# Two interleaved attention and MLP layers on one core: unpinned norms in the MLP, weight copies moved into attention, more buffers for projected tiles, another order of the first loads

## The chip, the cores and the metric

The kernel runs on one core of a Trainium2 chip. The metric is the device time of one execution in microseconds. The kernel before took 3666.28 us (median of 3 runs, 3660.68 to 3670.13).

The engines are named as in the profile: PE is the matrix engine (TensorE), PEld its weight loads, DVE the vector engine, ACT the scalar engine, POOL is GpSimd, and SP only issues DMAs. ACT and POOL issue some DMAs too. Each engine works through its own instructions in a fixed order and waits on semaphores.

## The reference

The input x has 2048 rows of 512 numbers in float32. Two layers follow each other, with the same weights in both:

```python
def _A_ref(x, wqkv, wo):                 # 32 heads of 16
    q, k, v = split_heads(x @ wqkv)
    scores = q @ k.T * 16 ** -0.5
    return heads_to_rows(softmax(scores) @ v) @ wo
def _B_ref(x, w1, b1, w2):
    h = x @ w1 + b1                      # 512 -> 1792
    sp = log1p(exp(-abs(h))) + where(h > 0, h, 0)
    return (h * tanh(sp)) @ w2
x = x + _A_ref(_layernorm(x), A_wqkv, A_wo)
x = x + _B_ref(_layernorm(x), B_w1, B_b1, B_w2)
x = x + _A_ref(_layernorm(x), A_wqkv, A_wo)
x = x + _B_ref(_layernorm(x), B_w1, B_b1, B_w2)
```

(The helpers `split_heads` and `heads_to_rows` stand for reshapes and transposes.)

## The kernel before

**Numbers.** Matmul operands are kept as a high and a low part (two tiles of type float32r). A product is three matmuls: high by high, high by low, low by high (`mm3`, L153, whose matmuls appear in the profile as L156, L157, L158). A part pair is made by a copy on ACT and a subtraction on DVE (`split_psum`, L149; profile lines L150 and L151) or, for weights, by a copy on ACT and a subtraction on POOL (`split_load`, L105; L112, L113).

**Stages.** The 2048 rows are four chunks `c` of 512. Per layer:

1. *Norm* (`norm_parts`, L163). Statistics on DVE (L174, L175), the inverse root on POOL (L171, tile `rs`), the normalised rows `xn` (L187, DVE), four transposes per 128 rows on PE (L198, tile `tp`), and the split of the transposed tile into `th` and `tl`. A norm is a generator of five pieces: the statistics, then one piece per 128 rows. Names that end in q belong to attention's norms, names that end in m to the MLP's.
2. *Projections* (`qkv`, L445). For each of 8 column blocks `m` (0 to 3 for queries, 4 to 7 for keys) and each chunk `c`, 12 matmuls of 128x512 fill a PSUM bank; ACT and DVE split it into the tile `pt`, and ACT issues its 512 KB write to the DRAM tensor `scr` (L471). The order of the pairs (m, c) is a list (L676). `pt` has three buffers, under the tag raw. When all (0, c) and (4, c) are written, `prep_qk` (L238) loads the tiles `ks` and `qs` of the first group of heads from `scr`, half of it through SP and half through POOL. From block 6 on, `some_max` (L450) puts score matmuls `pm` (L292) and their row maxima `mxv` (L296, DVE) between the projections. Then come the V projections (`v_parts`, L492), whose result goes to DRAM and comes back as `va`.
3. *Attention* (`run`, L394), 512 steps: scores again (`sp`, `ss`), exponentials on ACT into the tiles `p` (L347, L357), the products with V (`pv`, L372), and, 28 steps ahead, the maxima. Functions in a dictionary `hooks` run after a given step. In layer 0 the weights of the later stages are split there on POOL and copied to DRAM (`split_keep`, L119).
4. *Output projection and MLP* (`wo_parts`, `mlp`). `mlp` walks over 56 pairs (c, f), f being one of 14 column blocks of 128. `hid(c, f)` (L584) does 12 matmuls and a chain of eleven instructions: `hb` (ACT, L594), `he` (DVE, L595), `he` (ACT, L596), `he` (DVE, L597), `hr` twice (ACT, L598, L599), `hb` (POOL, L600), `ah` (DVE, L602), `hb` (POOL, L603), `al` (DVE, L604). `outp` (L607) runs two pairs later (LAG) and does 12 matmuls on `ah` and `al` into `mo`. `hb` has two buffers, `he` and `hr` one.

Norms of the next chunk, and in the last chunk of layer 0 the first three norms of layer 1's attention, run beside the MLP: `spread` (L206) hangs their five pieces behind the `hid` of five neighbouring f. Layer 1's projection weights are loaded there too (L769, through ACT's queue).

**Weights.** `load_qkv` (L432) in layer 0 loads raw weights (tag raw, three buffers, shared with `pt`; the V weights use a tile of their own, `rawv`) and splits them; `keep_all` (L654) copies the split weights to DRAM through POOL, 1 MB each, from where layer 1 loads them. Weights 0 and 2 serve blocks 0, 1, 4, 5; weights 1 and 3 serve blocks 2, 3, 6, 7; weights 4 and 5 are V.

**Space.** Nearly all large tiles (`x`, `th`, `tl`, split weights, `ks`, `qs`, `va`, `p`, `v`) share one tag of 22 slots of 8 KB per partition (`b8`, L76).

**What sets the order.** The program is traced in Python; then a list scheduler plays a timing model (L778) and fixes each engine's order of instructions and which buffer a tile gets: of the instructions that are ready in the model, the one traced first goes first. `behind` (L160) pins an instruction behind the one traced just before it on its engine. In `spread` every DVE and ACT instruction of a norm is pinned (`pin=behind`); its transposes on PE and its `rs` on POOL are not.

Of the kernel before, what the change touches and what calls it, by code (L numbers as in the profile page):

```python
# [9 lines left out]
F32 = mybir.dt.float32  # L10
F32R = mybir.dt.float32r
BF16 = mybir.dt.bfloat16
AF = mybir.ActivationFunctionType
ALU = mybir.AluOpType
# [4 lines left out]
P = 128  # L19
S, D, H, DH, F = 2048, 512, 32, 16, 1792  # L20
NCH = 4
CW = S // NCH
# [17 lines left out]
AHEAD = 24  # L40
PRE = 4
FILL = 12
GSTEPS = NCH * NKT
STEPS = NG * GSTEPS
HEADS = STEPS * HG
# [7 lines left out]
def kernel(ctx: ExitStack, tc: tile.TileContext, x, wqkv, wo, w1, b1, w2, out):  # L53
    nc = tc.nc
# [5 lines left out]
    tmp = ctx.enter_context(tc.tile_pool(name="tmp", bufs=2))  # L60
# [15 lines left out]
    def b8(shape, dt, name):  # L76
        return blk.tile(shape, dt, tag="blk", name=name)
# [18 lines left out]
    def t512(tag, name, dt=F32):  # L96
        return tmp.tile([P, 512], dt, tag=tag, name=name, bufs=T_BUFS.get(tag, 2))

    kept, unkept = {}, []

    def keep(key, t):
        kept[key] = dram.tile(list(t.shape), F32R, name="w" + key)
        nc.gpsimd.dma_start(kept[key].bitcast(F32), t.bitcast(F32))

    def split_load(key, src, a, b, later, raw=None):  # L105
        t = b8([P, 2, a, b], F32R, "s" + key)
        if raw is None:
            raw = tmp.tile([P, a, b], F32, tag="raw", name="r" + key, bufs=3)
        nc.sync.dma_start(raw, src)

        def split():
            nc.scalar.activation(t[:, 0], raw, AF.Copy)  # L112
            nc.gpsimd.tensor_tensor(t[:, 1], raw, t[:, 0].bitcast(F32), op=ALU.subtract)  # L113
            unkept.append((key, t))

        later.append(split)
        return t
# [28 lines left out]
    def rows2(w, j):  # L146
        return w[ts(j, 2 * P), :].rearrange("(k p) n -> p k n", p=P), 2, w.shape[1]
# [9 lines left out]
            pe(nc.tensor.matmul(acc, ah, bl, start=False, stop=False))  # L157
            pe(nc.tensor.matmul(acc, al, bh, start=False, stop=last and i == n - 1))  # L158

    def behind(ins):  # L160
        return tc.keep_in_program_order(ins)

    def norm_parts(src, nm, got, key, tag, fine=False, pin=lambda ins: ins, pe=lambda ins: ins, halves=False):  # L163
        st = tmp.tile([P, NCH, 6], F32, tag="st", name=f"st{nm}")
        mv = tmp.tile([P, NCH, 2], F32, tag="mv", name=f"mv{nm}")
        ve = tmp.tile([P, NCH], F32, tag="ve", name=f"ve{nm}")
        rs = tmp.tile([P, NCH], F32, tag="rs", name=f"rs{nm}")

        def rstd(t, n):
            pin(nc.vector.tensor_scalar(ve[:, t : t + n], mv[:, t : t + n, 1], EPS, None, op0=ALU.add))  # L170
            nc.gpsimd.tensor_tensor(rs[:, t : t + n], ve[:, t : t + n], mhalf[:, t : t + n], op=ALU.pow)  # L171

        for t in range(NCH):
            pin(nc.vector.bn_stats(st[:, t], src[:, t]))  # L174
            pin(nc.vector.bn_aggr(mv[:, t], st[:, t]))  # L175
            if fine:
                rstd(t, 1)
        if not fine:
            rstd(0, NCH)
        yield  # L180
        th = b8([P, KT, CW], F32R, f"th{nm}")
        tl = b8([P, KT, CW], F32R, f"tl{nm}")
        got[key] = (th, tl)
        for t in range(NCH):
            xn = t512("f", f"xn{nm}{t}")
            pin(
                nc.vector.tensor_scalar(  # L187
                    xn, src[:, t], mv[:, t, 0:1], rs[:, t : t + 1], op0=ALU.subtract, op1=ALU.mult
                )
            )  # L190
            if halves:
                yield
            if tag == "mx":
                tp = ps.tile([P, 2, 512], F32, tag=tag, name=f"tp{nm}{t}")[:, 0]
            else:
                tp = pbank(tag, f"tp{nm}{t}")
            for k in range(KT):
                pe(nc.tensor.transpose(tp[:, ts(k, P)], xn[:, ts(k, P)], ident))  # L198
            split_psum(th[:, :, ts(t, P)], tl[:, :, ts(t, P)], tp.rearrange("p (k n) -> p k n", k=KT), pin)
            yield  # L200
# [3 lines left out]
            pass  # L204

    def spread(hooks, at, src, nm, got, key):  # L206
        parts = norm_parts(src, nm, got, key, "acc", pin=behind)
        for c, f in at:
            hooks.setdefault((c, f), []).append(lambda: next(parts, None))

    class Attention:
# [60 lines left out]
        def max_mm(self, s, half):  # L272
# [3 lines left out]
            g, qb = divmod(b, NCH)  # L276
            u, i = divmod(2 * i + half, GSTEPS // 4)
            qt, n = divmod(i, NCH)
            l = self.l
            if half == 0 and s % GSTEPS >= GSTEPS // 2 and g + 1 < NG:  # L280
                if s % GSTEPS == GSTEPS // 2:
                    self.parts = self.prep_qk(g + 1)
# [111 lines left out]
        def run(self, hooks, pre, fill):  # L394
# [49 lines left out]

    def qkv(l, wts, tt, order, late, due):  # L445
        scr = [dram.tile([2, P, S], F32R, name=f"scr{l}{m}") for m in range(2 * NCH)]
        att = Attention(l, scr)
        ahead = [0]

        def some_max():  # L450
            if ahead[0] < AHEAD + PRE:
                att.tick()
                for n in range(2):
                    att.max_mm(ahead[0], n)
                ahead[0] += 1

        done = 0
        for m, c in order:
            if c not in tt:
                late()  # L460
            w = wts[m // 2]
            pt = tmp.tile([P, 2, CW], F32R, tag="raw", name=f"pt{l}{m}{c}", bufs=3)
            th, tl = tt[c]
            acc = pbank("s", f"qk{l}{c}{m}")
            mm3(
                acc,
                [(w[:, 0, k, ts(m % 2, P)], w[:, 1, k, ts(m % 2, P)], th[:, k], tl[:, k]) for k in range(KT)],
                pe=att.pe,
            )
            split_psum(pt[:, 0], pt[:, 1], acc)  # L470
            nc.scalar.dma_start(  # L471
                scr[m][:, :, ts(c, CW)].bitcast(F32).rearrange("a p n -> p a n"), pt.bitcast(F32)
            )
            for fn in due.get((m, c), []):
                fn()
            if m in (0, 4):
                done += 1
                if done == 2 * NCH:
                    for _ in att.prep_qk(0):
                        pass  # L480
                    att.chained = True
            elif done == 2 * NCH and m in MAX_M:
                some_max()
        i = 0
        for c in range(NCH - 1):
            for _ in v_parts(l, c, wts, tt, att, False):
                i += 1
                if i % 3 == 0:
                    some_max()
        return att  # L490
# [154 lines left out]
        return xc  # L645

    wts, tt, late = {}, {}, None
    splits = []

    def split_all():  # L650
        while splits:
            splits.pop(0)()

    def keep_all():  # L654
        while unkept:
# [5 lines left out]
    for c in range(NCH):  # L661
        parts = norm_parts(xc[c], f"q0{c}", tt, c, "mx", c == 0)
        next(parts)
        if c == 0:
            split_all()
        for _ in parts:
            pass
        if c == 0:
            load_qkv(0, wts, (1, 3), splits)
            split_all()  # L670
        if c + 2 < NCH:
            xc.append(load_x(c + 2))
    for l in range(2):
        due = {}
        if l == 0:
            order = [(0, 0), (4, 0), (1, 0), (5, 0), (0, 1), (4, 1), (1, 1), (0, 2), (4, 2), (0, 3), (4, 3)]  # L676
            due[1, 2] = [lambda: load_qkv(0, wts, (4, 5), splits)]
            due[2, 0] = [split_all]
            due[6, 0] = [keep_all]
        else:  # L680
            order = [(0, 0), (0, 1), (0, 2), (4, 0), (4, 1), (4, 2), (1, 0), (1, 1), (1, 2), (5, 0), (0, 3), (4, 3)]
        order += [(m, c) for m in (1, 5, 2, 6, 3, 7) for c in range(NCH) if (m, c) not in order]
# [17 lines left out]
        def at(s, fn):  # L700
            hooks.setdefault(s, []).append(fn)

        if l == 0:
            jobs = [(f"wo{i}", rows2(wo, i)) for i in range(2)]
            jobs += [(f"w1{i}", cols(w1, i)) for i in range(7)] + [(f"w2{i}", rows2(w2, i)) for i in range(7)]
            for i, (key, src) in enumerate(jobs):
                split_keep(hooks, 20 + 26 * i, key, *src)
# [57 lines left out]
        wts, tt = {}, {}  # L765
# [38 lines left out]
```

## Time and profile before

| what | us |
|---|---|
| median of 3 runs | 3666.28 |
| the profiled execution | 3669.02 |
| its span | 3667.2 |
| PE busy (28784 matmuls) | 3568.3 (97%) |
| DVE busy | 2968.4 (81%) |
| ACT busy | 2522.6 (69%) |
| POOL busy | 567.0 (15%) |
| layer 0: projections and V until attention is under way | 0 to about 214 |
| layer 0: attention | to about 1470 |
| layer 0: MLP, chunks end at | 1600, 1691, 1772, 1868 |
| layer 1: projections and attention | to about 3297 |
| layer 1: MLP, chunks end at | 3426, 3516, 3598, 3664 |

How to read it: a row of a timeline has start, duration, engine, line, operation, written tile <- read tiles, shapes, and in brackets how long the engine had been idle and who ended that. A window's row has, after its length, the busy time of PE, PEld, DVE, ACT and POOL with the number of instructions, then the granted clock of PE (1.00 is full speed), the mean share of the 16 DMA engines that was busy, and the GB/s that they moved. The end of a chunk is the end of its last addition to x (L621).

### The profile page before, as it was taken

What the parts mean: (1) busy time and instruction counts of PE and PEld (TensorE: products, weight loads), DVE (VectorE), ACT (ScalarE), POOL (GpSimd) and SP (SyncE); (2) the same over time, 40 slices, a digit from 0 to 9 for tenths busy, and PEclk for the clock granted to TensorE, in tenths of its full rate; (3) what the DMA queues carried; (4) which work ended last, traced back from release to release, by engine and by line L of the source; (5) the groups of instructions that cost most, each with busy time, mean ns of one, the idle gap of its engine ahead of it and who ended that gap; (6) DMA issues with size and microseconds to landing.
All of it is one profiled execution on the core that took longest, in us unless ns stands there. A gap on an engine that the chain in (4) does not pass through costs nothing. (4 is left out here: it accounts for less than half of the span.)

```text
span 3667.2 us, 69407 instructions
## 1 busy us (share of the span) xinstructions
PE 3568.3 (97%) x28784; PEld 1950.0 (53%) x28784; DVE 2968.4 (81%) x2978; ACT 2522.6 (69%) x3475; POOL 567.0 (15%) x589
## 2 busy tenths in 40 slices
PE   7999999999999999999889999999999999999999
PEld 6644444444444444877666444444444444447777
DVE  4779999999999994656647799999999999945565
ACT  2168888888888887344421788888888888873444
POOL 2200101001010002444430000000000000024455
PEclk9999999999999999999999999999999999999999
DMA  7641313313121124500154311112021221246000
GB/s 226 211 109 36 80 47 72 67 38 77 48 62 48 51 77 68 177 35 12 46 172 162 74 31 34 37 39 43 19 45 28 45 40 25 77 75 192 13 12 24
DMA packets 128707, 254.07 MB, mean 69 GB/s; under 512 B 18680, under 2 KB 62584, under 8 KB 114568
## 3 DMA queue, kind: packets, MB, share of 16 engines
q1 hardware_dynamic: 101896, 174.58, 19.5%
q0 software_dynamic: 8224, 35.21, 3.5%
q10 hardware_dynamic: 18272, 39.85, 2.9%
q8 instruction: 226, 3.70, 0.4%
q14 instruction: 89, 0.73, 0.1%
HBM read 148.38 MB, written 99.09 MB: 67 GB/s over the span
## 5 line engine op out<-in xcount | busy, mean ns | idle before, releaser
L296 DVE TENSOR_REDUCE mxv<-pm 128x2 f32<-128x1024 f32 x2048 | 2389.0, 1220 | 181.1 <-PE pm L292 132.4
L347 ACT ACTIVATE p<-sp 128x1024 f32<-128x1024 f32 x1366 | 1397.3, 1023 | 19.4 <-PE sp L346 12.0
L372 PE MATMUL pv<-p,va 128*32 128x128 f32 (+3 forms) x16048 | 1166.9, 392 | 0.0
L292 PE MATMUL pm<-ks,qs 48*128 48x512 f32 x4096 | 1109.1, 446 | 0.2
L357 ACT ACTIVATE p<-ss 128x512 f32<-128x512 f32 x1364 | 815.2, 598 | 384.7 <-PE ss L356 288.7
L346 PE MATMUL sp<-qs,ks 50*128 50x512 f32 x2732 | 739.6, 446 | 4.8 <-ACT p L347 3.3
L292 PEld LDWEIGHTS pm<-ks,qs 48*128 48x128 f32 x4096 | 460.7, 184 | 360.9 <-issue 236.6
L372 PEld LDWEIGHTS pv<-p,va 128*32 128x32 f32 x16048 | 368.3, 108 | 499.0 <-issue 418.4
L356 PE MATMUL ss<-qs,ks 50*128 50x512 f32 x1364 | 611.9, 449 | 0.1
L356 PEld LDWEIGHTS ss<-qs,ks 50*128 50x128 f32 x1364 | 252.0, 185 | 305.7 <-ACT p L357 210.1
L346 PEld LDWEIGHTS sp<-qs,ks 50*128 50x128 f32 x2732 | 277.0, 183 | 202.4 <-ACT p L347 117.6
L319 POOL CAST np<-nf 16x128 fp32r<-16x128 f32 x64 | 17.9, 280 | 2335.9 <-ACT nf L318 2317.8
L603 POOL TENSOR_TENSOR hb<-hb,hr 128x512 f32<-128x512 f32 x112 | 161.6, 1442 | 159.5 <-DVE ah L602 135.7
L600 POOL TENSOR_TENSOR hb<-hb,he 128x512 f32<-128x512 f32 x112 | 155.5, 1389 | 194.1 <-DVE he L597 192.7
L594 ACT ACTIVATE hb<-h,b1t 128x512 f32<-128x512 f32 x112 | 77.0, 687 | 152.8 <-DVE al L604 117.0
L604 DVE TENSOR_TENSOR al<-hb,ah 128x512 fp32r<-128x512 f32 x112 | 112.7, 1007 | 81.9 <-POOL hb L603 81.9
L598 ACT ACTIVATE hr<-he 128x512 f32<-128x512 f32 x112 | 70.8, 632 | 133.1 <-POOL hb L603 76.5
L150 ACT ACTIVATE pt<-qk 128x512 fp32r<-128x512 f32 x64 | 37.9, 597 | 176.9 <-PE qk L158 117.2
L596 ACT ACTIVATE he<-he 128x512 f32<-128x512 f32 x112 | 70.8, 632 | 95.2 <-DVE he L595 95.2
L602 DVE TENSOR_TENSOR ah<-hb,hr 128x512 fp32r<-128x512 f32 x112 | 76.9, 686 | 54.9 <-ACT hr L599 45.3
L597 DVE SCALAR_TENSOR_TENSOR he<-he 128x512 f32<-128x512 f32 x112 | 79.1, 706 | 49.4 <-ACT he L596 46.7
L595 DVE TENSOR_SCALAR he<-hb 128x512 f32<-128x512 f32 x112 | 67.6, 604 | 59.0 <-ACT hb L594 28.5
(225 smaller groups left out, 3289.3 us busy)
## 6 DMA issues: line engine op xcount, KB each, us to landing
scr<-pt ACTq DMA_DIRECT2D x64, 512.0 KB
qs<-scr SPq DMA_DIRECT2D x180, 128.0 KB
ks<-scr SPq DMA_DIRECT2D x180, 128.0 KB
vscr<-v SPq DMA_DIRECT2D x32, 512.0 KB
va<-vscr SPq DMA_DIRECT2D x64, 256.0 KB
oscr<-ot SPq DMA_DIRECT2D x64, 256.0 KB
ww<-sw POOLq DMA_DIRECT2D x14, 1024.0 KB, 5.2
qs<-np SPq DMA_DIRECT2D x512, 2.0 KB
```

What stands on the lines that cost most here:

```text
L292: nc.tensor.matmul(pm[:, e], qs[u][rows, q0 : q0 + P], ks[u][rows, ts(n, 512)], start=True, stop=True)
L296: nc.vector.tensor_reduce(self.mxs[b][:, 2 * u : 2 * u + 2, qt, n], pm, axis=AX.X, op=ALU.max)
L346: self.pe(nc.tensor.matmul(sp[:, e], k, q, start=True, stop=True))
L347: nc.scalar.activation(self.pts[-1][:, 0:n], sp[:, 0:n], AF.Exp, scale=SCALE)
L356: self.pe(nc.tensor.matmul(sp, k, q, start=True, stop=True))
L357: nc.scalar.activation(self.pts[i // 3][:, 2], sp, AF.Exp, scale=SCALE)
L372: nc.tensor.matmul(self.accs[b][ts(h, VW), cols], self.va[b // NCH][:, kt, h, :], self.pts[j][:, e, cols], start=kt == 0 and q0 == 0, stop ...
L594: nc.scalar.activation(hb, acc, AF.Identity, bias=b1t[:, f : f + 1])
L597: nc.vector.scalar_tensor_tensor(e, e, 2.0, e, op0=ALU.add, op1=ALU.mult)
L600: nc.gpsimd.tensor_tensor(hb, hb, e, op=ALU.mult)
L603: nc.gpsimd.tensor_tensor(hb, hb, r, op=ALU.mult)
L604: nc.vector.tensor_tensor(al, hb, ah.bitcast(F32), op=ALU.subtract)
```

## The change

Four things change.

*Norms.* In `spread`, the norm pieces are no longer pinned.

*Copies to DRAM.* `keep` pins its DMA behind what was traced before it on POOL. `keep_all` no longer runs in the projections (behind the first splits, and after pair (6, 0)) but as a hook of attention's step KEEP = 2, for all six weights together.

*Buffers.* Every other `pt` no longer comes from the three buffers of tag raw, but is half of a slot of the 22.

*First loads.* Loads and splits of `split_load` are pinned on SP, ACT and POOL. Weights 1 and 3 are loaded after pair (4, 0), the second projection, instead of right after the first norm, and split after (0, 3), the tenth; the V weights are loaded after (4, 2), the ninth, and split after (5, 2), the fifteenth, instead of after (1, 2) and (2, 0).

```diff
+KEEP = 2
...
     def keep(key, t):
         kept[key] = dram.tile(list(t.shape), F32R, name="w" + key)
-        nc.gpsimd.dma_start(kept[key].bitcast(F32), t.bitcast(F32))
+        behind(nc.gpsimd.dma_start(kept[key].bitcast(F32), t.bitcast(F32)))
...
-        nc.sync.dma_start(raw, src)
+        behind(nc.sync.dma_start(raw, src))
 
         def split():
-            nc.scalar.activation(t[:, 0], raw, AF.Copy)
-            nc.gpsimd.tensor_tensor(t[:, 1], raw, t[:, 0].bitcast(F32), op=ALU.subtract)
+            behind(nc.scalar.activation(t[:, 0], raw, AF.Copy))
+            behind(nc.gpsimd.tensor_tensor(t[:, 1], raw, t[:, 0].bitcast(F32), op=ALU.subtract))
             unkept.append((key, t))
...
     def spread(hooks, at, src, nm, got, key):
-        parts = norm_parts(src, nm, got, key, "acc", pin=behind)
+        parts = norm_parts(src, nm, got, key, "acc")
...
-        for m, c in order:
+        spare = []
+        for n, (m, c) in enumerate(order):
...
-            pt = tmp.tile([P, 2, CW], F32R, tag="raw", name=f"pt{l}{m}{c}", bufs=3)
+            if n % 2:
+                if not spare:
+                    two = b8([P, 2, 2, CW], F32R, f"pt{l}{m}{c}")
+                    spare += [two[:, 0], two[:, 1]]
+                pt = spare.pop(0)
+            else:
+                pt = tmp.tile([P, 2, CW], F32R, tag="raw", name=f"pt{l}{m}{c}", bufs=3)
...
         if c == 0:
-            split_all()
+            split_all(splits)
         for _ in parts:
             pass
-        if c == 0:
-            load_qkv(0, wts, (1, 3), splits)
-            split_all()
...
-            due[1, 2] = [lambda: load_qkv(0, wts, (4, 5), splits)]
-            due[2, 0] = [split_all]
-            due[6, 0] = [keep_all]
+            due[4, 0] = [lambda: load_qkv(0, wts, (1, 3), splits)]
+            due[4, 2] = [lambda: load_qkv(0, wts, (4, 5), later)]
+            due[0, 3] = [lambda: split_all(splits)]
+            due[5, 2] = [lambda: split_all(later)]
...
         if l == 0:
+            at(KEEP, keep_all)
```

More of the change, by code (lines that the diff above doesn't have):

```diff
@@ L97, in t512, with behind @@
         return tmp.tile([P, 512], dt, tag=tag, name=name, bufs=T_BUFS.get(tag, 2))
+    def behind(ins):
+        return tc.keep_in_program_order(ins)
     kept, unkept = {}, []
@@ L158, in mm3 @@
             pe(nc.tensor.matmul(acc, al, bh, start=False, stop=last and i == n - 1))
-    def behind(ins):
-        return tc.keep_in_program_order(ins)
     def norm_parts(src, nm, got, key, tag, fine=False, pin=lambda ins: ins, pe=lambda ins: ins, halves=False):
@@ L647, with split_all @@
     wts, tt, late = {}, {}, None
[L648 to L652, printed above, removed]
+    splits, later = [], []
+    def split_all(todo):
+        while todo:
+            todo.pop(0)()
     def keep_all():
```

## The prediction

> **What bounds the kernel now.** I read the page first, then PE's timeline for every gap of over a quarter of a microsecond, then the other engines' timelines around each gap, and the windows for stage totals. The strip of 40 slices says where to look:
>
> ```profile
> PE   7999999999999999999889999999999999999999
> DVE  4779999999999994656647799999999999945565
> PEclk9999999999999999999999999999999999999999
> ```
>
> TensorE (PE) is the bound nearly everywhere: in the attention stretches each 100 us window shows it 99.2 to 99.4 us busy. The page's PE row, 3568.3 of 3667.2 us, leaves 98.9 us idle. My list of gaps puts 27.9 us of it before 200 us, 35.0 between 1400 and 2060, and 13.0 after 3230. The diff touches exactly these places. (The digit of the clock strip is too coarse; the windows below show the clock.)
>
> The projections of layer 0:
>
> ```profile
> 34.23 0.60 ACT L150 ACTIVATE pt<-qk 128x512 fp32r<-128x512 f32 x1 [6.27 <-DMA scr<-pt]
> 36.75 1.94 PE L198 MATMUL tpq<-ident,xnq 128*128 128x128 f32 x8 [5.89 <-DVE tlq L151]
> 95.69 0.60 ACT L150 ACTIVATE pt<-qk 128x512 fp32r<-128x512 f32 x1 [8.26 <-DMA scr<-pt]
> 97.06 0.79 PE L156 MATMUL qk<-thq,sqkv 128*128 128x512 f32 x1 [4.50 <-DVE pt L151]
> 30.00:47.00 17.00, 10.42 (x41) 8.50 (x40) 10.00 (x19) 4.44 (x8) 0.00 (x0) 0.70 0.45 177
> 85.00:104.00 19.00, 11.52 (x31) 8.36 (x31) 2.77 (x4) 4.65 (x7) 3.04 (x3) 0.73 0.91 264
> ```
>
> ACT stands still because a `pt` buffer (three in tag raw) is still being written to DRAM. Everything behind it on ACT stands too, and PE follows. The seventh figure of a window (0.70, 0.73) is the granted clock: after such a gap, matmuls start 0.43 us apart instead of 0.23.
>
> The MLP, first in its last chunk of layer 0, then in an undisturbed place:
>
> ```profile
> 1801.15 0.69 DVE L604 TENSOR_TENSOR al<-hb,ah 128x512 fp32r<-128x512 f32 x1 [1.40 <-POOL hb L603]
> 1801.76 0.54 DVE L187 TENSOR_SCALAR xnq<-x,mvq,rsq 128x512 f32<-128x512 f32 x1
> 1802.60 0.43 DVE L595 TENSOR_SCALAR he<-hb 128x512 f32<-128x512 f32 x1 [0.30 <-ACT hb L594]
> 1801.88 0.69 ACT L594 ACTIVATE hb<-h,b1t 128x512 f32<-128x512 f32 x1 [2.92 <-DVE al L604]
> 1612.65 1.77 DVE L604 TENSOR_TENSOR al<-hb,ah 128x512 fp32r<-128x512 f32 x1 [1.19 <-POOL hb L603]
> 1772.00:1868.00 96.00, 79.76 (x341) 58.70 (x340) 56.29 (x106) 37.70 (x60) 34.71 (x27) 0.98 0.24 88
> ```
>
> A pinned norm piece (`xnq`) must follow `al`, the last step of an activation chain, and here the next chain starts only after it: chains stand one behind the other. `al` comes every 7.4 us (1793.73, 1801.15, 1808.57). Undisturbed (1604 to 1628), two chains overlap, `al` comes about every 5.3 us, and PE, which needs 24 x 0.227 = 5.45 us per step, is 25.00 of 25.00 us busy. So a norm in the MLP turns a PE-bound step into a chain-bound one. PE has two steps of slack (LAG); the fourth or fifth such step stalls it.
>
> **The change, part by part.** The sum is made against the profiled execution, 3669.0 us (span 3667.2), which lies 2.7 us above the median of 3666.3.
>
> *A. First stall, 30 to 47 us.* Idle 5.89 + 0.69. Slow clock: two batches of eight transposes at 1.94 instead of 1.04 us (1.8), and about ten matmuls 0.2 us late each (2.0). Together 10.4. More `pt` buffers take the ACT wait away. The four copies of weights to DRAM (4 MB, issued at 14.96 and 22.82) that the fourth `pt` had to share the DMA engines with are gone from here; SP now issues x before the second weights. POOL loses two 2.4 us subtractions ahead of the norm of chunk 1 (its `rsq` stood until 21.82). What is late next: the transposes of chunk 1 go in two batches through two PSUM buffers, with an ACT and a DVE copy between, some 2.4 us. **-8**.
>
> *B. Second stall, 85 to 104 us.* Idle 2.98 + 4.50; slow clock 6 + 15 matmuls x 0.2 = 4.2; together 11.7. Here the loads of `ks` and `qs` (issued 72 to 85, landing in 9 to 13 us) share the DMA engines with the `pt` writes; a write issued at 79.16 frees its buffer at 95.6. Sixteen microseconds are six projections of 2.73 us: three buffers fail, seven or more suffice. But the first score matmul needs `ks`. Before, 23 us passed from the last needed write (72.1) to the last landing (about 95). After, nine projections (24.5 us) lie between, with denser writes. I give 4 us back. **-7.7**; bounds 0 and -11.7.
>
> The staged weights 1 and 3 hold two of three raw buffers while projections 2 to 9 run, so every other `pt` has one buffer and 5.5 us to come back. A write issued at 70.4 had landed by 72.1; with 1.4 us from ACT to issue this fits, at nothing. If it took the 10.5 us of the first write (23.7 to 34.2), A would be lost.
>
> *The moved loads and splits.* SP issues weights 1 and 3 behind x2 and x3 (they took 7.8 us of SP's time at 5.15, waiting for a raw buffer) and the V weights ahead of the `ks` issues instead of behind them (87.44): two half-megabyte loads each, the first near 25 us, where four copies no longer are, the second near 55, where the DMA share was 0.55. ACT gets two copies of 1.06 us after projection (0, 3), with three PSUM banks as cover: 5 us of projections against 2.1. POOL subtracts 2 x 2.4 us ahead of its half of the `ks` issues, done some 7 us after that projection; the last needed write lands some 6 us after it (2.73 + 1.4 + 1.7), so POOL's issues come 1 us late, inside the 4 us of B. The V splits go behind those issues; their first reader stood at 147. Nothing more for these; without the PSUM cover it would be 2 us.
>
> *C. Layer 1 projections.* PE waits for `pt` 2.20 + 1.69 + 1.80 us (1917 to 1927). Weights live six slots here as before, and the norm inputs are gone, so the extra buffers have room. **-5.5**.
>
> *D. First MLP chunk, both layers.* Layer 0: 0.39 + 2.75 + 0.90 + 0.67 idle, and 1576 to 1592 at clock 0.89 (1.8 lost): 6.5. Layer 1: 0.39 + 2.75 + 0.69, and 3400 to 3417 at 0.80 (3.4 lost): 7.2. Unpinned, statistics can go where DVE idles (9.5 of 20 us in 1580 to 1600) and `xn` need not follow `al`. I take four fifths: **-11**.
>
> *E. Last chunk of layer 0.* Three norms stand in it; 96.0 - 79.8 = 16.2 us idle. The norms add 12 x (0.54 + 0.69) + 3 x 3.4 = 25 us of DVE work to 14 steps, 1.8 us each; with the 3.5 us of an undisturbed step DVE reaches 5.3 of the 6.0 us that PE then needs. It fits, barely, so I take two thirds: **-11**.
>
> *F. Middle chunks, both layers.* Gaps of 3.9 us each; half: **-4**.
>
> *G. Copies moved into attention.* Six copies issue on POOL behind what is traced there (0.57 us each, 3.4 in all); queued behind them is the next `np`, which has 50 us. They land in 5.2 us (`ww`, in attention) to 9.1 us (`wqkv`, before) each, 31 to 55 us in series, and until then four to six of 22 slots stay taken as the first `p` tiles need them. Fourteen copies of that size already run in layer 0's attention with PE at 99.2%; six at once the trace does not show. Between 0 and 15 us (31 us at half speed) I take **+3**, near the row of attention.
>
> Sum: -8 - 7.7 - 5.5 - 11 - 11 - 4 + 3 = -44.2, or 3624.8 on the profiled execution, **3622** on the median.
>
> [...] A 2.98 us gap at 85.2 was followed by matmuls 0.43 us apart from 89.80 on. [...]
>
> `al` took 1.77 us beside POOL's multiply at 1612.58, and 0.69 us at 1801.15 with POOL idle. [...]
>
> **Rivals.**
> 1. *The pins cost nothing of their own.* The overlapped `al` is 1.1 us longer; with norms that makes 5.3 + 1.1 = 6.4 us of DVE per step, over PE's 6.0, and D to F bring little. Against: 1604 to 1629 is full in spite of the collisions. -21 + 3: about 3648.
> 2. *The load of `ks` is the bound.* B is given back in full at the first score matmul, the rest stands: 3630.
> 3. *Slower: norm copies in ACT's queue wait for PE.* The instruction order is fixed at compile time from modelled times. If a copy of a transposed tile stands ahead of an activation, and its transpose stands behind an output matmul that waits for that activation's chain, each piece costs up to the longest gap before an output matmul, 2.75 us at 1582. Nine spread norms have 36 pieces: 99 us for the 38 lost now (D to F), +61, less 18 from A, B, C and G: 3709. It decides above (38 + 18) / 36 = 1.6 us a piece. At 1579.76 such a copy delayed the next activation by only 0.6 us.
>
> **How the numbers follow.** Forecast 0.60 (3600 to 3644); rival 1 0.18, rival 2 0.12, rival 3 0.10. Everything recovered (10.4 + 11.7 + 5.7 + 13.7 + 18, E with its clock of 0.98, + 7.8) is 67: 3599, so the range starts at 3598. It ends at 3656, where the MLP gives nothing and half of the projections' gain is gone; that leaves out rival 3 and part of rival 1. A measurement can tell about 0.3%, 11 us. Faster by more: 0.60 + 0.14 + 0.11 = 0.85; within: 0.04 + 0.01 + 0.03 = 0.08; slower: 0.07.
>
> **What would show it.** A, B: no ACT wait on `scr<-pt` before 105 us, clock 1.00 after 25 us, attention starting 12 to 20 us earlier. D, E: `al` every 5.3 to 6.2 us in norm stretches, the last chunk of layer 0 in 83 to 88 us instead of 96. G: PE near 99% in the first 100 us of attention. It is wrong if `al` still comes every 7 us, or PE waits for `ks` or for `p` for over 10 us.

## The result and the profile after

The changed kernel takes 3619.99 us (median of 4 runs, 3618.25 to 3625.20), beside 3667.55 us for the kernel before in the same session (4 runs): a ratio of 0.9876, 95% interval 0.9858 to 0.9893, or about 46 us less. Predicted were 3622, with 3598 to 3656 as the range. The profiled execution took 3625.2 us (span 3623.4), 43.8 us less than the profiled one before; the sum of the prediction's terms was -44.2. The lines of the changed kernel lie 1 to 8 further down in the file (`al` is L612, `xn` L188, the copies and subtractions of `pt` L154 and L155).

The page's strip first. Two of its 40 digits for PE were 8 before, for the slices from 1742 to 1925 us; now only the first slice is below 9:

```profile
PE   7999999999999999999999999999999999999999
```

The strip can't show the projections. PE's timeline does, with ACT's longest wait ahead of a `pt` copy and the write that ACT issues just before it, then the same two windows as before:

```profile
15.88 1.94 PE L199 MATMUL tpq<-ident,xnq 128*128 128x128 f32 x8 [5.08 <-DVE tlq L155]
18.51 1.65 PE L160 MATMUL qk<-thq,sqkv 128*128 128x512 f32 x3 [0.69 <-ACT thq L154]
38.55 1.08 PE L199 MATMUL tpq<-ident,xnq 128*128 128x128 f32 x4 [2.34 <-DVE mvq L176]
85.84 0.80 PE L160 MATMUL qk<-thq,sqkv 128*128 128x512 f32 x1 [3.08 <-DVE pt L155]
84.00 0.37 ACTq L479 DMA_DIRECT2D scr<-pt  x1
84.47 0.60 ACT L154 ACTIVATE pt<-qk 128x512 fp32r<-128x512 f32 x1 [9.23 <-DMA qs<-scr]
30.00:47.00 17.00, 12.88 (x55) 9.97 (x55) 11.67 (x26) 5.17 (x10) 1.77 (x2) 0.80 0.09 33
85.00:104.00 19.00, 18.16 (x74) 13.95 (x75) 8.57 (x11) 6.03 (x10) 6.55 (x3) 0.91 0.89 268
```

The waits of 5.89 and 4.50 us are gone, but three gaps of over 2 us are left behind the first transposes: 5.08 us at 15.88, before the first projection (2.89 before, and 2.90 in a second profile of the changed kernel, e12 below), a new one of 2.34 at 38.55, behind statistics of a later chunk, and 3.08 at 85.84, where one of 2.98 stood before. The first window went from 10.42 to 12.88 busy microseconds at a clock of only 0.80; the second from 11.52 to 18.16.

The MLP's last chunk of layer 0, DVE's timeline and the window from chunk end to chunk end:

```profile
1783.09 0.68 DVE L612 TENSOR_TENSOR al<-hb,ah 128x512 fp32r<-128x512 f32 x1
1783.69 0.42 DVE L603 TENSOR_SCALAR he<-hb 128x512 f32<-128x512 f32 x1
1784.03 0.54 DVE L188 TENSOR_SCALAR xnq<-x,mvq,rsq 128x512 f32<-128x512 f32 x1
1789.61 0.68 DVE L612 TENSOR_TENSOR al<-hb,ah 128x512 fp32r<-128x512 f32 x1
1755.00:1843.00 88.00, 82.55 (x373) 64.62 (x372) 50.93 (x91) 39.42 (x63) 32.20 (x25) 1.00 0.30 108
```

The row `xnq` now stands behind the next chain's `he` instead of ahead of it, and `al` comes every 6.52 us instead of every 7.4. The chunk takes 87.7 us instead of 96.3.

**Where the time went**, from the milestones of the two profiles (each is the start of the first matmul of its kind, or an end):

| stretch | before | after | difference | predicted |
|---|---|---|---|---|
| to the end of the 12th `pt` copy on ACT | 70.0 | 69.8 | -0.2 | -8 (A) |
| from there to the first score matmul | 35.6 | 28.5 | -7.1 | -7.7 (B) |
| first score matmul to the first `h`, layer 0 (attention) | 1389.3 | 1388.4 | -0.9 | +3 (G) |
| first `h` to the end of the MLP, layer 0 | 372.9 | 356.3 | -16.6 | about -18 (D, E, F) |
| to the first attention step of layer 1 | 149.8 | 144.6 | -5.2 | -5.5 (C) |
| attention, layer 1 | 1303.0 | 1302.7 | -0.3 | 0 |
| MLP, layer 1 | 346.6 | 333.1 | -13.5 | about -8 (D, F) |

### The profile page after: what moved, and what is told of

Its sections match the earlier page's. It is cut to its first block, busy times and chain, and to the rows that moved or that the text cites. A ratio compares the mean times of both kernels' runs of the same rounds, so it can differ in the third digit from the quotient of the medians.

```text
span 3623.4 us, 69472 instructions
## 1 busy us (share of the span) xinstructions
PE 3553.0 (98%) x28784; PEld 1948.5 (54%) x28784; DVE 2963.7 (82%) x2978; ACT 2520.7 (70%) x3475; POOL 567.6 (16%) x589
## 5 line engine op out<-in xcount | busy, mean ns | idle before, releaser
L373 PEld LDWEIGHTS pv<-p,va 128*32 128x32 f32 x16048 | 368.2, 108 | 498.2 <-issue 417.8
L612 DVE TENSOR_TENSOR al<-hb,ah 128x512 fp32r<-128x512 f32 x112 | 108.0, 964 | 84.5 <-POOL hb L611 82.2
L154 ACT ACTIVATE pt<-qk 128x512 fp32r<-128x512 f32 x64 | 37.9, 598 | 158.9 <-PE qk L162 127.5
```

The costliest lines, as they stand in the source:

```text
L373: nc.tensor.matmul(self.accs[b][ts(h, VW), cols], self.va[b // NCH][:, kt, h, :], self.pts[j][:, e, cols], start=kt == 0 and q0 == 0, stop ...
L612: nc.vector.tensor_tensor(al, hb, ah.bitcast(F32), op=ALU.subtract)
```

## The experiments

Since the end of layer 0's MLP overlaps the projections of layer 1, the table adds these two stretches ("MLP 0 + projections 1": first `h` of layer 0 to the first attention step of layer 1). The time from the first score matmul to the first attention step was 87.9 us in all but one of these profiles (88.4), and attention 1299 to 1302 and 1300 to 1304 us; they are left out. Medians and ratios are against the kernel before in the same session; the stretches come from one profile each.

| kernel | first projection at | 12th `pt` copy ends | first score matmul | MLP 0 + projections 1 | MLP 1 | median | ratio, 95% |
|---|---|---|---|---|---|---|---|
| before | 16.2 | 70.0 | 105.6 | 522.7 | 346.6 | 3667.55 | |
| changed | 18.5 | 69.8 | 98.3 | 501.0 | 333.1 | 3619.99 | 0.9876, 0.9858 to 0.9893 |
| e1_norms_pinned | 18.6 | 68.9 | 97.9 | 521.8 | 347.1 | 3657.99 | 0.9981, 0.9971 to 0.9990 |
| e2_only_unpinned | 16.4 | 69.7 | 102.8 | 500.8 | 334.3 | 3630.53 | 0.9908, 0.9892 to 0.9925 |
| e7_pin_rows | 17.2 | 67.4 | 96.3 | 523.5 | 341.2 | 3651.38 | 0.9958, 0.9943 to 0.9973 |
| e8_pin_rest | 18.5 | 70.0 | 97.8 | 503.6 | 336.4 | 3627.16 | 0.9895, 0.9880 to 0.9909 |
| e3_three_buffers | 17.1 | 71.2 | 103.7 | 503.6 | 333.5 | 3634.56 | 0.9918, 0.9903 to 0.9933 |
| e4_only_buffers | 18.5 | 67.4 | 106.5 | 524.4 | 346.0 | 3667.16 | 1.0006, 0.9996 to 1.0015 |
| e6_old_loads | 17.2 | 63.7 | 104.2 | 498.1 | 335.0 | 3628.24 | 0.9896, 0.9880 to 0.9913 |
| e5_copies_early | 17.1 | 67.3 | 94.6 | 498.2 | 334.4 | 3620.88 | 0.9877, 0.9862 to 0.9892 |
| e9_first_norms | 23.3 | 92.0 | 118.7 | 499.7 | 333.9 | 3646.15 | 0.9936, 0.9923 to 0.9948 |
| e10_split_later | 14.1 | 65.5 | 93.3 | 498.0 | 333.7 | 3618.09 | 0.9866, 0.9850 to 0.9881 |
| e11_both_first | 20.7 | 90.3 | 118.4 | 497.6 | 333.6 | 3640.17 | 0.9923, 0.9911 to 0.9936 |
| e12_same_again | 16.8 | 68.4 | 95.1 | 499.4 | 333.2 | 3622.94 | 0.9887, 0.9870 to 0.9903 |

### The pins in the MLP: e1, e2, e7, e8

Two kernels take the pins alone. e1 is the changed kernel with its norms pinned again:

```diff
-        parts = norm_parts(src, nm, got, key, "acc")
+        parts = norm_parts(src, nm, got, key, "acc", pin=behind)
```

> The changed kernel with the norm pieces in the MLP pinned again, all else as changed. My theory (a pinned piece puts the activation chains one behind the other): the two MLPs lose again what they gained in the trace, 16.6 us in layer 0 (first hidden matmul to the end of the last chunk: 356.3 instead of 372.9) and 13.5 us in layer 1, so about 3650 us, and the rows of al come every 7.4 us in the last chunk of layer 0. Rival (the pins cost nothing of their own, the MLP gained through slots that the other edits free): at most a few microseconds over 3620.

e2 is the kernel before with that one line changed the other way, and nothing else.

> The kernel before with nothing changed but the norm pieces in the MLP unpinned. My theory: the MLP gain does not need the other edits, -30 us: about 3637, with the projections' two stalls (5.9 us at 31, 3.0 and 4.5 us near 90) still there. Rival (it needs freed slots): well under -15 us.

Pinned again, the MLP has its old lengths: 521.8 and 347.1 us. Unpinned alone it has the new ones: 500.8 and 334.3. So this one line is worth 34.8 us read from e1 and 34.2 from e2, of some 44, and the other three edits change neither stretch by more than a few microseconds. The layer 1 projections gain nothing from the buffers while the norms are pinned (e1 521.8, e4 524.4, before 522.7).

e7 and e8 split the pins. In e7 only the normalised rows are pinned, in e8 all but these:

```diff
-            pin(
+            xpin(
...
-        parts = norm_parts(src, nm, got, key, "acc")
+        parts = norm_parts(src, nm, got, key, "acc", xpin=behind)
```

> The changed kernel with only the row instruction xn of each MLP norm piece pinned; statistics and splits are free. My theory: xn behind al is what puts the chains in a row, since the transposes and the copies follow from it: at least 20 of the 30 us come back, 3640 to 3650. Rival (it is the statistics or the copies on ACT): under 10 us, 3620 to 3630.

> The changed kernel with statistics and splits of each MLP norm piece pinned, and the row instruction xn free. My theory: little comes back, 3620 to 3630. Rival: the splits' pins (the copy on ACT behind the chain's last activation, the subtraction on DVE behind al) are the cause, 3640 to 3650.

The rows' pin brings back 22.5 us in the first stretch (523.5 against 501.0) and 8.1 of 14 in layer 1; all other pins together bring back 2.6 and 3.3 (in the last chunk of layer 0 alone they cost 6.5 us, 94.2 against 87.7, and its first chunk, 102.7 against 105.0, and the projections win part of that back). DVE's timeline of e7 in the last chunk of layer 0 is that of the kernel before:

```profile
1780.16 0.69 DVE L613 TENSOR_TENSOR al<-hb,ah 128x512 fp32r<-128x512 f32 x1 [1.40 <-POOL hb L612]
1780.77 0.54 DVE L189 TENSOR_SCALAR xnq<-x,mvq,rsq 128x512 f32<-128x512 f32 x1
1781.61 0.43 DVE L604 TENSOR_SCALAR he<-hb 128x512 f32<-128x512 f32 x1 [0.30 <-ACT hb L603]
1787.57 0.69 DVE L613 TENSOR_TENSOR al<-hb,ah 128x512 fp32r<-128x512 f32 x1 [1.40 <-POOL hb L612]
```

The row sits between `al` and the next `he`, and `al` comes every 7.41 us. The row itself is half a microsecond of work; where it stands makes two chains serial. Unpinned, `he` goes first. The chains still hardly overlap in this chunk (6.52 us, not the 5.3 of an undisturbed place), but PE needs 5.9 us per step here (82.55 us busy in the window's 14 steps), so most of the idle time goes. Why layer 1 takes back only 8.1 of 14 us through the rows, these runs do not tell.

### The projections of layer 0: e3, e4, e6, e5

e3 is the changed kernel with three buffers for all `pt` (its edit follows); e4 is the kernel before with the new buffers and nothing else.

```diff
-            if n % 2:
...
-                pt = spare.pop(0)
-            else:
-                pt = tmp.tile([P, 2, CW], F32R, tag="raw", name=f"pt{l}{m}{c}", bufs=3)
+            pt = tmp.tile([P, 2, CW], F32R, tag="raw", name=f"pt{l}{m}{c}", bufs=3)
```

> The changed kernel with all projected tiles in the three buffers of tag raw, all else as changed. My theory: ACT waits for scr<-pt again. Layer 1 loses 5.4 us. In layer 0 weights 1 and 3 hold two of the three buffers for nine projections, so the loss there is larger than the 7.4 us that the projections gained: 10 to 20 us. In all 3635 to 3645. Rival (the gain of the projections comes from the moved copies and loads alone): layer 0 unchanged, 3625.

> The kernel before with nothing changed but every other projected tile in half of a slot. My theory: the first stall (31 to 37 us) and the second (85 to 97) go without the moved copies, since three buffers were what they waited for: score matmuls start 7 to 15 us earlier, layer 1's projections gain 5.4: 3647 to 3655. Rival (the copies to DRAM and the loads of x are what slows the first writes): the first stall stays in part, -5 to -8 us in all.

e6 is the changed kernel with the old loads: nothing of `split_load` pinned, weights 1 and 3 right after the first norm, V weights after (1, 2).

```diff
+        if c == 0:
+            load_qkv(0, wts, (1, 3), splits)
+            split_all(splits)
...
-            due[4, 0] = [lambda: load_qkv(0, wts, (1, 3), splits)]
-            due[4, 2] = [lambda: load_qkv(0, wts, (4, 5), later)]
-            due[0, 3] = [lambda: split_all(splits)]
-            due[5, 2] = [lambda: split_all(later)]
+            due[1, 2] = [lambda: load_qkv(0, wts, (4, 5), later)]
+            due[2, 0] = [lambda: split_all(later)]
```

> The changed kernel with loads and splits of the projection weights in the order of before and unpinned (weights 1 and 3 right after the first norm). My theory: the new order is what gave back the gain of the first stall. x2 and x3 arrive early, DVE does their statistics ahead of the rows of chunk 1, and both first subtractions on POOL stand against two row instructions on DVE (2.6 us each instead of 0.55). So the old order starts the first projection near 16.2 instead of 18.5 us and the score matmuls 0 to 6 us earlier: 3614 to 3620. Rival (the two raw buffers and POOL time that the early weights take matter more): 3623 to 3630.

None of the three brings the first score matmul near the changed kernel's 98.3 us: 103.7, 106.5, 104.2. (e2, whose program up to there is the kernel before's, has 102.8 beside its 105.6; so 3 us is what two profiles of one program can differ by.) With the new buffers and the old loads (e4, e6) the 12th copy ends 2.7 and 6.3 us earlier than before; only the second is clearly more than profiles of one program differ by. Then all of it is lost in one gap. ACT's and PE's timelines of e4:

```profile
93.97 0.60 ACT L150 ACTIVATE pt<-qk 128x512 fp32r<-128x512 f32 x1 [17.64 <-DMA scr<-pt]
95.35 0.79 PE L156 MATMUL qk<-thq,sqkv 128*128 128x512 f32 x1 [12.31 <-DVE pt L151]
```

and of e6, with what ACT does before:

```profile
72.33 1.09 ACT L154 ACTIVATE pt<-qk 128x512 fp32r<-128x512 f32 x2 [5.88 <-DMA qs<-scr]
82.92 9.85 ACTq L479 DMA_DIRECT2D scr<-pt  x2
92.81 0.60 ACT L154 ACTIVATE pt<-qk 128x512 fp32r<-128x512 f32 x1 [19.39 <-DMA scr<-pt]
94.19 0.80 PE L160 MATMUL qk<-thq,sqkv 128*128 128x512 f32 x1 [14.74 <-DVE pt L155]
```

As far as the trace shows, more buffers would not end this gap by themselves. ACT works through its instructions in order: e6's late copy starts at 92.81 us, 0.04 us behind the issues of two writes (82.92 to 92.77) that stand ahead of it. The low parts of both tiles are ready at 74.27 us, but the writes are issued at 82.92 and at 92.40. What they wait for can be read from the trace's semaphore events, which the rows above don't show. The DMAs of ACT and SP share eight completion semaphores, and each late write is issued within 0.1 us of the landing of the transfer that used its semaphore before: at 82.92 a load of `ks` that SP had issued at 68.33, at 92.40 ACT's own write of 71.61, which took 20.7 us. e4 has the same pair, at 84.65 and 93.56. The changed kernel has one such issue, at 84.00, 0.08 us behind the landing of a load of `qs`. The kernel before has three (79.16, 86.36, 90.13, each 0.08 us behind the landing of a load of `qs` or `ks`), and of its longest wait, up to 95.69, the last 5 us are for a buffer. No run changes the semaphores, so this is read from the traces and not tested.

What fills the DMA engines then? The window from 70 to 85 us, and the trace's list of DMA issues from 60 to 100 us, of e6:

```profile
70.00:85.00 15.00, 9.45 (x42) 7.40 (x40) 1.29 (x2) 1.09 (x2) 2.44 (x5) 0.96 1.03 142
```

```profile
rawv<-in_A_wqkv_dram SPq DMA_DIRECT2D x2, 512.0 KB
```

and the same window of the changed kernel, in whose list no `rawv` stands:

```profile
70.00:85.00 15.00, 12.76 (x57) 10.23 (x55) 1.90 (x3) 1.73 (x3) 7.81 (x14) 1.00 1.04 258
```

The last two figures matter: both are full (1.03 and 1.04 of the 16 engines), but e6 moves 142 GB/s and the changed kernel 258; e4 moves 192, the kernel before and e3 230. In e6, e4 and the kernel before, SP issues the megabyte of V weights right behind its loads of `ks` and `qs`, at 78.91, 81.37 and 87.44 us; in the changed kernel it is issued at 15.30 and in e3 at 30.59. But the V weights did not begin e6's stall: from 69 to 78 us, before their issue, e6's engines are already full at 130 GB/s, and ACT's queue moves nothing. Why the same loads run at such different rates stays open. e3 has the early load and only three buffers, and stalls 8.77 us at 93.46; there ACT's copy does wait for a buffer, until 92.09. So this gain needs both edits: -1.9, +0.9 and -1.5 us for one without the other (e3, e4, e6), -7.4 for both. What in the order of loads matters is not shown. The edit moves the V weights, the weights 1 and 3, and with them which transfers share a semaphore, and no run moves one of these alone.

e5 puts the copies to DRAM back into the projections, after pair (6, 0), not pinned, and leaves the rest of the change:

```diff
-        behind(nc.gpsimd.dma_start(kept[key].bitcast(F32), t.bitcast(F32)))
+        nc.gpsimd.dma_start(kept[key].bitcast(F32), t.bitcast(F32))
...
+            due[6, 0] = [keep_all]
...
-            at(KEEP, keep_all)
```

> The changed kernel with the copies of the weights to DRAM unpinned and traced in the projections again (behind pair (6, 0)), so that they may issue as soon as a split is done. My theory: the copies were no cause of the projections' stalls once there are more buffers, and in attention they cost nothing: within 4 us of 3620. Rival (the copies share the DMA engines with the writes of projected tiles): the first 100 us lose 5 to 10 us, about 3627.

3620.88 us, as the changed kernel. In its trace the copies are issued at 15.89, 70.98, 76.83 and 92.80 us, and the first score matmul is not later (94.6). Where the copies stand makes no difference that these runs can tell. In attention they cost nothing either: of the first 100 us PE is busy 98.43 us with them (98.45 before), though POOL issues all six at once:

```profile
175.61 3.22 POOL L107 DMA_DIRECT2D wqkv<-sqkv  x6
```

### The first norms: e9, e10, e11

Why did the first stretch gain nothing in the changed kernel, though ACT no longer waits? Two suspects stand in its trace: statistics of later chunks ahead of the rows that PE waits for (2.34 us at 38.55), and rows that take 2.5 us instead of 0.54 at the start. e9 pins the four first norms. e10 traces the split of the first weight behind the second of the first norm's four row pieces, and that of the second weight behind the fourth, instead of both ahead of the rows; so it moves them by more than the one piece that its expectation names. e11 does both.

```diff
-        parts = norm_parts(xc[c], f"q0{c}", tt, c, "mx", c == 0)
+        parts = norm_parts(xc[c], f"q0{c}", tt, c, "mx", c == 0, pin=behind)
```

> The changed kernel, with the statistics, rows and copies of layer 0's four first norms pinned in the order of the program. After the change TensorE still waits 2.34 us at 38.55, behind statistics of chunk 1 or later (mvq), and 0.7 to 1.35 us at four more places before 52 us; the first projection starts at 18.51. Theory (the order of DVE's norm work costs the gain of the first stall): the gaps between 30 and 52 us shrink by 2 to 4 us, and the first score matmul comes 2 to 4 us earlier, about 3616 to 3618. Rival 1 (the load of ks takes whatever is won ahead of it): the projections up to 85 us come earlier, the gap before the first score matmul grows by the same amount, and the time stays within 2 us of 3620. Rival 2 (the statistics of later chunks were free work, and pinned they come too late): gaps grow at the second and third norm, 3 to 6 us slower.

```diff
+        for i, _ in enumerate(parts):
+            if c == 0 and i == 1:
+                splits.pop(0)()
         if c == 0:
             split_all(splits)
-        for _ in parts:
-            pass
```

> The changed kernel, with the first weight split traced one norm piece later, so that POOL's subtractions do not come beside the first four rows of normalised x. After the change two of these rows take 2.59 and 2.56 us instead of 0.54 beside POOL's subtractions at 10.02 and 12.33, and TensorE waits 5.08 us at 15.88. Theory (the shared access of DVE and POOL delays the start): rows of 0.54 us, first projection 1.5 to 4 us earlier than 18.5, and if nothing takes it back the time falls by as much. Rival 1 (the load of ks takes it back): first projection earlier, first score matmul no earlier than in the changed kernel. Rival 2 (the subtraction itself is on the path, because the third matmul of a product needs the low part of the weights): rows of 0.54 us, but the first projection waits for the subtraction and starts at 18 to 21.

> The changed kernel with both edits: the four first norms pinned, and the first weight split traced one norm piece later. Theory (the start and the order of the norm work each cost on their own): the two gains add, 3 to 7 us earlier at the first score matmul, about 3613 to 3617. Rival (the load of ks sets the first score matmul): the same time as the changed kernel to within 2 us, with a longer gap ahead of the first score matmul.

e9 is 26 us slower than the changed kernel (22 in the profiles): the theory was wrong in its sign, and the second rival's direction right, its size far too small. The timelines of DVE and PE:

```profile
17.18 0.69 DVE L155 TENSOR_TENSOR tlq<-tpq,thq 128x512 fp32r<-128x512 f32 x1 [1.84 <-ACT thq L154]
17.78 0.54 DVE L188 TENSOR_SCALAR xnq<-x,mvq,rsq 128x512 f32<-128x512 f32 x1
20.83 0.54 DVE L188 TENSOR_SCALAR xnq<-x,mvq,rsq 128x512 f32<-128x512 f32 x1
18.47 1.09 PE L199 MATMUL tpq<-ident,xnq 128*128 128x128 f32 x4 [1.96 <-DVE xnq L188]
```

A pinned row waits for the `tl` of the row before it, which waits for ACT's copy and PE's transposes: one row goes all the way round before the next starts, 3.05 us each. It is the MLP's pattern again: the pin turns a pipeline into a ring. So the free order, with statistics of later chunks ahead and its gap of 2.34 us, is the cheaper of the two.

e10 is the other suspect. DVE and POOL of the changed kernel:

```profile
10.07 5.07 DVE L188 TENSOR_SCALAR xnq<-x,mvq,rsq 128x512 f32<-128x512 f32 x2 [0.56 <-POOL rsq L172]
10.02 4.83 POOL L117 TENSOR_TENSOR sqkv<-rqkv,sqkv 128x1024 fp32r<-128x1024 f32 x2
```

and of e10:

```profile
9.92 0.55 DVE L188 TENSOR_SCALAR xnq<-x,mvq,rsq 128x512 f32<-128x512 f32 x1 [0.56 <-POOL rsq L172]
11.07 0.54 DVE L188 TENSOR_SCALAR xnq<-x,mvq,rsq 128x512 f32<-128x512 f32 x1
12.31 2.36 POOL L117 TENSOR_TENSOR sqkv<-rqkv,sqkv 128x1024 fp32r<-128x1024 f32 x1 [2.41 <-ACT sqkv L116]
```

With the subtractions behind them the rows take 0.55 us, and the first projection starts 4.4 us earlier than in the first profile of the changed kernel and 2.6 earlier than in its second (e12, below). At the first score matmul 4.9 and 1.7 us of that are left: the load of `ks` takes back none or a third. That DVE and POOL share an access, as the expectation has it, no run shows; shown is how long the rows take with a subtraction beside them and without. e11 starts 2.6 us earlier than e9, but its score matmul comes at the same time. In whole runs e10's 3618.09 us and the changed kernel's 3619.99 and 3622.94 can't be told apart: the intervals of their ratios overlap. It is the lowest median of the study, and below the changed kernel by less than 0.15%.

### The same program again: e12

The changed kernel itself, with a second profile.

> The changed kernel itself, once more, with a second profile: how far do two executions of one program differ stage by stage? Its four times so far run from 3618.25 to 3625.2 us, and the one with the profile was the slowest. In that profile a gap of 1.99 us at 1860.30 was followed by eight transposes in 1.94 us and a matmul of 0.80; in the version with the later first split the same gap was followed by 1.22 and 0.50. Theory (the clock that TensorE is granted after a short gap differs from one execution to the next): the second profile has the same gaps to 0.3 us, but other matmul durations behind some of them, and its stages differ from the first one's by 1 to 4 us at the boundary of the layers and in the projections, under 1 us in the norm-free stretches. The first projection then starts at 18.5 again, since the rows of x beside POOL's subtractions are in the program. Rival (the stage lengths are the program's, and the version with the later split really gains 2.7 us at the boundary): the second profile repeats 501 us from the first h of layer 0 to the first sp of layer 1 within 1 us, and the eight transposes take 1.9 us again.

It tells how much a stretch of one profile is worth. The first projection starts at 16.77 instead of 18.51 us: 2.90 us of idle time ahead of the second transposes instead of 5.08, so the rows beside POOL's subtractions are not simply "in the program", as I had expected. In the kernel before, one row started at 9.78, 0.13 us ahead of a subtraction at 9.91, and took 0.55 us; in the changed kernel's first profile it started at 10.07, 0.05 us behind one at 10.02, and took 2.59 us. The draw is not the change's: e4, whose order up to there is that of the kernel before, starts at 18.5 us too. Between the short row and the long one lies 0.18 us, measured from the start of the subtraction. And the same gap at the boundary of the layers has another clock behind it, as the theory had it (499.4 us instead of 501.0, and 1.23 us for the eight transposes, so the rival is out). First profile, then the second, then that of e10:

```profile
1860.30 1.94 PE L199 MATMUL tpq<-ident,xnq 128*128 128x128 f32 x8 [1.99 <-DVE tlq L155]
1862.92 0.80 PE L160 MATMUL qk<-thq,qkv0l 128*128 128x512 f32 x1 [0.69 <-ACT thq L154]
```

```profile
1857.03 1.23 PE L199 MATMUL tpq<-ident,xnq 128*128 128x128 f32 x8 [1.99 <-DVE tlq L155]
1858.94 0.79 PE L160 MATMUL qk<-thq,qkv0l 128*128 128x512 f32 x1 [0.69 <-ACT thq L154]
```

```profile
1855.92 1.22 PE L199 MATMUL tpq<-ident,xnq 128*128 128x128 f32 x8 [1.99 <-DVE tlq L155]
1857.84 0.50 PE L160 MATMUL qk<-thq,qkv0l 128*128 128x512 f32 x1 [0.69 <-ACT thq L154]
```

Over 1855 to 1875 us the granted clock was 0.83, 0.91 and 1.00. So differences of some 3 us in one profile's stretches are no more than the draw of a run. The 20 us of the pins stand far above that. Loads and buffers do too, by the number of profiles: the seven with both edits and free first norms have the first score matmul at 93.3 to 98.3 us, the five without one or both at 102.8 to 106.5. Of the seven, e1, e7, e8 and e12 run the changed kernel's own order up to there, so the changed kernel has five profiles of this stretch: first projection at 16.8 to 18.6 us, 12th copy at 67.4 to 70.0, first score matmul at 95.1 to 98.3.

## Why the prediction was right, and where it was not

The time, the sign and the sum were right (-44.2 predicted, -43.8 in the profile), and terms that were off in opposite directions helped: A gave 7.8 us less than forecast, G and layer 1's MLP 3.9 and 5.5 us more. That the sum came within half a microsecond is luck.

**A, first stall: wrong in this kernel.** The wait went, as predicted, but -8 became -0.2, and between 0.0 and -2.6 in the five profiles with this order. The step that failed is "what is late next: the transposes of chunk 1 ..., some 2.4 us". Late next were also the statistics at 38.55 (2.34), and three gaps of 0.74, 0.87 and 1.35 us up to 51.44; the clock in the window stayed at 0.80. The later start (+2.3 in this profile) is a draw, as e12 and e4 show. e6 shows in its one profile that up to 6.3 us were there to be had, with another order of loads. Two of the prediction's own signs failed: the clock was not 1.00 after 25 us (0.80 and 0.91 in the two windows), and attention started 7.4 us earlier, not 12 to 20.

**B, second stall: the size right, the mechanism only in part.** -7.1 against -7.7 in this profile. But "three buffers fail, seven or more suffice" does not hold by itself: in e4 and e6 the new buffers do not suffice, because ACT stands at the issue of its writes. In the kernel before, too, ACT's waits of 4.65 and 6.61 us, up to 79.63 and 86.83, end with such an issue. The term had credited the load order with nothing, and had put the V weights near 55 us, where they came at 15.30; that the size came out is in part luck. Rival 2 (the load of `ks` takes it back) was wrong for the changed kernel, and right in kind for e4 and e6, where the writes stand behind these loads.

**C, layer 1's projections: right size, mostly another cause.** The three `pt` waits of 5.7 us in all became one of 2.74, but a wait of 1.99 us for the fourth norm is new. Buffers without unpinning gave nothing (e1, e4); unpinning without buffers gave all of it within the spread (e2 500.8, changed 501.0 and 499.4). With free norms the buffers are worth at most 6 us (e3 503.6, against 498 to 501).

**D, E, F, the MLP: the mechanism right, the sizes off.** In layer 0 -16.6 against about -18, in layer 1 -13.5 against about -8, and the rows' pin as the main cause is shown by e7 and e8. The last chunk of layer 0 gave -8.6 where E had -11. What was mis-sized in layer 1 are the slow clock and the shares taken. The first chunk of layer 1 before, and after:

```profile
3320.00:3426.00 106.00, 101.96 (x440) 82.40 (x439) 60.97 (x88) 44.76 (x67) 45.74 (x38) 0.97 0.33 106
```

```profile
3290.00:3395.00 105.00, 104.24 (x465) 85.29 (x464) 67.30 (x98) 46.16 (x70) 52.27 (x42) 1.00 0.33 102
```

In 105 us the chunk now runs 465 matmuls instead of 440 in 106: 25 matmuls more, at 0.227 us 5.7 us of the next chunk's work done ahead; so the gain shows at the next chunk's end (that chunk takes 80.2 us instead of 90.1). I had taken four fifths of what was lost in the first chunk and half in the middle one. More came than the 11.1 us that I had counted as lost in layer 1 (7.2 + 3.9): of the 13.5 us, 7.4 are PE's idle time (12.7 before, 5.3 after), and 6.1 are shorter busy time of the same 1441 matmuls, where I had counted 3.4 for the slow clock. "`al` every 5.3 to 6.2 us" was too much to hope for: 6.52 in the last chunk of layer 0, at 87.7 us for the chunk (83 to 88 forecast).

**Rival 1** (in overlapping chains `al` is longer again): it is. `al` still takes 1.77 us in places (at 3389.76 and 3411.66, beside POOL's `hb` from 3389.69 and 3411.58; 0.68 at 3394.91, with POOL idle), but on average 964 ns, below the 1007 before, and it did not decide.

**Rival 3** (norm copies make ACT wait for PE): it is there, and was nearer than I thought. Ten times in the last chunk of layer 0, ACT's copy of a transposed tile waits for PE, 0.93 to 1.60 us each, and the next chain stands behind it; the point from which I had it decide was 1.6 a piece. But these are waits of ACT, and PE's slack covers most of each.

**G, the copies: nothing instead of +3.** Both placements are free (e5, and the attention stretch, -0.9).

## What to carry to other kernels

Pinning an instruction of side work behind the main chain is not free because the instruction is short: half a microsecond in the wrong place made every step wait for the step before, and cost 35 us here, in two stages of the kernel alike. When an engine's wait ends on a DMA, look whether it stands at a buffer or at the issue of its own next DMA: more buffers paid here only together with another order of the loads, since without it ACT stood at two issues for 7 to 9 us each. And before reading 2 us out of a profile, take a second profile of the same program.

## What the hardware did that I had not expected

DVE's instruction for a normalised row (`xn`, float32) took 0.54 us with no subtraction on POOL beside it and 2.5 us beside one (in the changed kernel 5.07 us for two, the subtractions 4.83 for two). The idle time ahead of the first projection differs between executions of one program: ahead of the second transposes PE stood idle for 5.08 us in the changed kernel's first profile and for 2.90 in its second. By the start of the row, the one that started 0.13 us ahead of a subtraction (kernel before) took 0.55 us, and the one 0.05 us behind (changed kernel) 2.59. A third shows how rough the starts are: in e1 a row that by the profile started 0.05 us ahead (10.09 against 10.14) took 2.69 us. What holds a row up is not shown.

The granted clock over the 20 us around a gap of 1.99 us (1855 to 1875) was 0.83, 0.91 and 1.00 in three executions with the same gap (the changed kernel twice, and e10), and the eight transposes behind it took 1.94, 1.23 and 1.22 us. What sets the clock there is not shown.

Full DMA engines need not mean bytes: 1.03 of them busy moved 142 GB/s in e6, and 1.04 moved 258 in the changed kernel.
